# Scores of the first eight attention jobs in the float32 mode, weights in two strided transfers, and early v on GpSimd's queue

## The chip, the cores and the metric

The program runs on one NeuronCore of a Trainium2 chip. Its engines are PE (TensorE: matmuls; PEld are its weight loads), DVE (VectorE), ACT (ScalarE), POOL (GpSimd) and SP (SyncE), and transfers are issued on the queues of SP, ACT and POOL. The metric is the device time of one execution in microseconds; the time before is 1215.47 us, the median of 3 runs (1214.58 to 1215.83).

## The reference

Causal attention with a decay, over 8 batches of 8 heads, 576 positions and head size 64, all in float32; then a two-layer MLP with a squared ReLU on the 4608 tokens of width 512.

```python
scores = scale * np.matmul(q, k.transpose(0, 1, 3, 2))
cum = np.cumsum(np.log(np.clip(f, 0.0001, 1.0)), axis=-1)
scores = np.where(causal, -1e9, scores + cum[:, :, :, None] - cum[:, :, None, :])
attn = np.exp(scores - np.max(scores, axis=-1, keepdims=True))
attn = attn / (np.sum(attn, axis=-1, keepdims=True) + 1e-09)
x = np.matmul(attn, v)          # to [tokens, 512]
h = np.maximum(x @ w_in, 0.0)   # w_in 512 x 2048
out = h * h @ w_out             # w_out 2048 x 512
```

## The kernel before, in words

**Precision.** PE multiplies in one pass in a rounded mode (float32r) or, more slowly, in float32. Most products are made as three rounded ones: each operand is split into an upper (rounded) part and the rest, and upper x rest, rest x upper and upper x upper are added up in PSUM. The rounding copies and the subtractions that make the parts are work for ACT, DVE and POOL.

**Attention jobs** (the function `job`). Jobs 0 to 7 ("LOW") take two heads each of batches 0 and 1, and of them the first 256 positions. Jobs 8 to 23 ("HIGH") take one head each of the same batches, positions 256 to 575. The other 48 jobs ("FULL") take one whole head. A job loads q and k (`load`, ACT's queue) into a buffer, `raw`; copies q and k rounded to `r2` (c1) and `kl0` (c2), and, as the second operand pair, to `r1` and `l2` (c3, c4), which also get the rests from the subtractions s1, s2 (L607). `rows` brings the two parts of the cumulated decay by SP's queue. A rounded product of q and k (L687) gives each row's maximum on DVE (L695); the maximum goes as a column through a transfer on SP's queue (`up<-tcol`, L704) into a further row of the operand, so that the scores come out of PE with decay and maximum already in them: L739 (upper parts, with the three extra rows) and L743 (the rests, 128 rows). ACT takes the exponential (L749), POOL zeroes what lies above the diagonal (L752, the mask). In heads below `NWHOLE` the probabilities go into one float32 matmul with v (L824, which the profile shows as two records); in the others they are split (L777 on ACT, L780 on DVE) and go into three (L827, L828, L829). `finish` gathers the denominators of two jobs (`cmp<-den`, L901), inverts them on DVE (L905, L906), and spreads them by two more transfers.

**Weights** (`weight`). w_in and w_out come in 16 pieces each of 128 x 512 float64 numbers; a piece is loaded as int32 by POOL's queue (L420) and turned into float32 by one step on ACT (L423) and four on DVE (L427 to L444), then split into upper (L309, `w<-osb`) and rest (L452, the last step). The buffers of pieces 17 to 31 hold operands and v of the first jobs before.

**MLP** (`chunk`, `mlp`). 18 chunks of 256 tokens, 16 steps each. A chunk's x is split (L977, L983); a step is 12 matmuls of 256 columns (L1020), on ACT the ReLU (L1026) and the rounded square (L1035), a square (L1030 on ACT or L1032 on DVE), the rest (L1038 on DVE) and 6 matmuls of 512 columns (L1049). Chunks 0 and 1 start while weights still arrive: step n needs weights 2n and 2n+1.

**What sets the order.** All work is entered in a planner (class `Order`) with a priority, its needs, its buffers, and one or more engines with estimated costs; the planner runs through it in estimated time, takes for each engine the earliest, and writes down the order. Each engine then runs in exactly that order, and waits if an input is late. `SLACK` is a margin that the planner leaves behind each result, by the engine of the step that uses it. `job_prio` and `weight_prio` give the priorities.

Of the kernel before, what the change touches and what calls it, by code (L numbers as in the profile page):

```python
# [9 lines left out]
F32 = mybir.dt.float32  # L10
# [84 lines left out]
class Order:  # L95
# [6 lines left out]
    SLACK = {"PE": 250.0, "DVE": 200.0, "ACT": 200.0, "POOL": 200.0, "SP": 200.0}  # L102
# [19 lines left out]
    def run(self):  # L122
# [10 lines left out]
        while ready:  # L133
            best = {}
            for op in ready:
# [6 lines left out]
                else:  # L142
                    way = None
                    for w in op.ways:
# [4 lines left out]
                        if way is None or start + busy < way[0] + way[1][1]:  # L149
                            way = start, w  # L150
                    start, w = way
# [15 lines left out]
            if e in queue and path == "dma":  # L167

                queue[e] = max(queue[e], start + 600) + lag
                end = queue[e] + 1900  # L170
# [44 lines left out]
def decay_attention_relu2_kernel(  # L215
# [40 lines left out]
    NWHOLE = 16  # L256
# [15 lines left out]

# [61 lines left out]
    spare_v = []  # L334
    for i in (17, 18, 19):
        x = spare(i, F32)[:, :12 * (D + 2)].rearrange("p (g i j d) -> p g i j d", g=3, i=2, j=2)
        spare_v += [x[:, g] for g in range(3)]
    spare_v = spare_v[:NLOW]
# [71 lines left out]
    def weight(i):  # L410
# [7 lines left out]
        def stage(e):  # L418
            raw_w[i] = wk.tile([P, 2 * DM], I32, name=f"w{i}", bufs=1)
            nc.gpsimd.dma_start(out=raw_w[i], in_=(w_in, w_out)[i % 2][i // 2].bitcast(I32))  # L420
# [40 lines left out]
        elif 20 <= i < 24:  # L461
            after += [(x, g) for x in splits for g in range(RAWS)]
# [3 lines left out]
        add(w("stage"), [dma(8 * P * DM, "POOL")], stage, after, prio=p)  # L466
# [56 lines left out]
    def job(g):  # L523
# [37 lines left out]
        def rows(e):  # L561
# [4 lines left out]
            elif g == 0:  # L566
                for i, c in enumerate(cum):
                    nc.sync.dma_start(out=kl0[D + i:D + i + 1, :2 * QA].bitcast(F32), in_=c[:2, :QA])
# [52 lines left out]
        rp = [("ch", QA), ("cl", QA)] if g == 0 else [("cum", 0), ("cum", 1)]  # L621
        add(("c1", g), [act(nq)] if kind != LOW and b < 2 else [dve(nq)], c1, start, take=[operands], give=give, prio=p)
        add(("rows", g), [dma(20000, "SP", 1 if g else 2)], rows, [("c1", g)] + rp, prio=p)
        add(("c2", g), [act(nk)] if b < 2 else [dve(nk), act(nk)], c2, [("load", g), ("c1", g)], give=give, prio=p)
        add(("c3", g), [act(nk), dve(nk)], c3, [("load", g), ("c1", g)], give=give, prio=p + 0.1)
# [520 lines left out]
```

## Time and profile before

| | |
|---|---|
| median of 3 runs | 1215.47 us |
| profiled execution: its time, its span | 1220.14 us, 1218.4 us |
| busy in the span: PE, DVE, ACT, POOL | 1165.4, 790.8, 724.4, 381.0 us |
| first matmul, first MLP matmul | 9.94 us, 63.77 us |
| last weight ready (last L452 starts) | 247.4 us |

Times are in microseconds unless marked ns. A row of windows gives the stretch, its length, the busy time of PE, PEld, DVE, ACT and POOL with their instruction counts, the granted PE clock (1.00 is full), the busy share of the 16 DMA engines and GB/s; a stretch before the first change of the clock is given as 1.00 whatever it was. A row of the timeline gives start, duration, engine, line, operation, output<-input, shapes, and in brackets the idle time before it and what ended it. A group's row gives count, busy time, mean ns of one, and idle time before it. Matmuls overlap: one's duration is longer than what it adds to PE; the chain of waits counts only what it adds.

### The profile page before, as it was taken

How to read it: one execution, taken by the hardware profiler on the slowest of the kernel's cores; microseconds unless marked ns; L12 is line 12 of the kernel's file. 1: busy time of each engine (PE TensorE's matmuls, PEld its weight loads, DVE VectorE, ACT ScalarE, POOL GpSimd, SP SyncE). 2: the span in 40 equal slices, each digit the busy share in tenths (PEclk: the TensorE clock that was granted, in tenths of full speed). 3: DMA queues.
4: the chain of work that ended last, by engine and by line, in shares of the span. 5: the costliest groups of instructions: out<-in, count | busy, mean ns of one | idle time of the engine just before them, and what ended most of it. 6: DMA issues, size and time to landing. Idle time of an engine off the chain costs nothing.

```text
span 1218.4 us, 23217 instructions
## 1 busy us (share of the span) xinstructions
PE 1165.4 (96%) x7600; PEld 1038.7 (85%) x7600; DVE 790.8 (65%) x2211; ACT 724.4 (59%) x1859; POOL 381.0 (31%) x568
## 2 busy tenths in 40 slices
PE   4679998999999999999999999999999999999998
PEld 4558776789998898999999998899998999999997
DVE  7689988968877677777657674467656753233332
ACT  3566766556766666767777674477746763333232
POOL 3223321245444344544444442045423510000000
PEclk9689999999999999999999999999999999999999
DMA  3654554321222112222212212012211200000000
GB/s 80 140 129 121 143 154 113 87 77 43 65 50 62 40 41 59 47 64 47 59 42 59 42 43 58 19 41 43 69 31 44 47 28 11 18 19 11 8 19 18
DMA packets 122354, 69.85 MB, mean 57 GB/s; under 512 B 101914, under 2 KB 106042, under 8 KB 122234
## 3 DMA queue, kind: packets, MB, share of 16 engines
q10 hardware_dynamic: 53760, 31.47, 10.5%
q1 hardware_dynamic: 63866, 20.12, 7.5%
q0 software_dynamic: 4608, 16.78, 4.4%
q8 instruction: 61, 1.00, 0.3%
q14 instruction: 59, 0.48, 0.1%
HBM read 58.14 MB, written 9.88 MB: 56 GB/s over the span
## 4 chain that ended last, share of the span: by engine, by line
PE 85%; DMA 6%; DVE 4%; ACT 2%; issue 1%; POOL 1%; SPq 0%; ACTq 0%; POOLq 0%; DVEq 0%
PE bank L1049 31%; PE bank L1020 30%; PE bank L739 4%; PE bank L687 4%; PE bank L743 4%; PE bank L824 3%; PE bank L829 3%; PE bank L828 3%; PE bank L827 3%; DMA den<-rdr 2%; DMA cmp<-den 1%; DMA rdr<-cmp 1%; DMA up<-tcol 1%; DVE bank L695 1%; POOL pl L752 0%
## 5 line engine op out<-in xcount | busy, mean ns | idle before, releaser
L1049 PE MATMUL bank<-w,gh 128*128 128x512 f32 x1152 | 413.5, 400 | 1.9 <-DVE w L452 1.9
L1020 PE MATMUL bank<-xh,w 128*128 128x256 f32 x2304 | 324.4, 283 | 2.5 <-DVE xh L977 1.1
L1020 PEld LDWEIGHTS bank<-xh,w 128*128 128x128 f32 x2304 | 302.3, 189 | 13.7 <-DVE xh L977 1.3
L1026 ACT ACTIVATE r<-bank 128x256 f32<-128x256 f32 x288 | 110.2, 383 | 243.3 <-PE bank L1020 220.7
L1049 PEld LDWEIGHTS bank<-w,gh 128*128 128x128 f32 x1152 | 218.0, 189 | 41.8 <-DVE w L452 2.3
L1049 PE MATMUL bank<-w,gl 128*128 128x512 f32 x576 | 228.6, 397 | 0.3 <-DVE gl L1038 0.3
L1032 DVE TENSOR_TENSOR g<-r 128x256 f32<-128x256 f32 x191 | 82.9, 434 | 174.6 <-ACT r L1026 173.3
L1020 PE MATMUL bank<-xl,w 128*128 128x256 f32 x1152 | 182.0, 280 | 0.9 <-DVE xl L983 0.9
L752 POOL TENSOR_SCALAR_AFFINE_SELECT p<-p 128x128 f32<-128x128 f32 (+1 forms) x240 | 84.3, 353 | 307.3 <-ACT p L749 302.0
L695 DVE CUSTOM_DVE_ANT_0 bank<-bank,mz 128x448 f32<-128x448 f32 (+4 forms) x320 | 137.1, 431 | 66.5 <-PE bank L687 64.9
L780 DVE TENSOR_TENSOR pl<-p,ph 128x320 fp32r<-128x320 f32 (+3 forms) x240 | 147.9, 625 | 39.5 <-ACT ph L777 38.4
L1038 DVE TENSOR_TENSOR gl<-g,gh 128x256 fp32r<-128x256 f32 x288 | 139.6, 485 | 51.9 <-ACT g L1030 20.3
L1020 PEld LDWEIGHTS bank<-xl,w 128*128 128x128 f32 x1152 | 155.3, 189 | 1.3 <-DVE xl L983 1.3
L607 POOL TENSOR_TENSOR st<-qkraw,up 64x576 fp32r<-64x576 f32 x96 | 146.2, 1523 | 27.3 <-issue 5.4
L749 ACT ACTIVATE p<-bank 128x320 f32<-128x320 f32 (+4 forms) x288 | 110.0, 389 | 56.5 <-DVE pl L780 30.6
L739 PE MATMUL bank<-up 67*128 67x192 f32 (+3 forms) x364 | 121.8, 335 | 20.4 <-DMA up<-tcol 10.3
L1035 ACT ACTIVATE gh<-r 128x256 fp32r<-128x256 f32 x288 | 120.1, 417 | 31.6 <-PE bank L1049 11.6
L777 ACT CAST ph<-p 128x320 fp32r<-128x320 f32 (+3 forms) x240 | 106.2, 446 | 49.0 <-POOL p L752 27.6
L687 PE MATMUL bank<-up 66*128 66x448 f32 (+1 forms) x352 | 112.1, 322 | 13.0 <-DMA up<-w 9.9
L1049 PEld LDWEIGHTS bank<-w,gl 128*128 128x128 f32 x576 | 109.4, 190 | 15.1 <-DVE gl L1038 1.5
L743 PE MATMUL bank<-st 128*128 128x192 f32 (+3 forms) x364 | 109.3, 302 | 0.0
L739 PEld LDWEIGHTS bank<-up 67*128 67x128 f32 (+1 forms) x364 | 68.5, 188 | 31.5 <-DVE cmp L905 7.2
(102 smaller groups left out, 1612.5 us busy)
## 6 DMA issues: line engine op xcount, KB each, us to landing
qkraw<-in_qk ACTq DMA_DIRECT2D x48, 288.0 KB
v<-in_v ACTq DMA_DIRECT2D x64, 160.0 KB
out<-osb SPq DMA_DIRECT2D x35, 256.0 KB
w<-in_w_in POOLq DMA_DIRECT2D x16, 512.0 KB, 4.4
w<-in_w_out POOLq DMA_DIRECT2D x16, 512.0 KB, 4.6
den<-rdr SPq DMA_DIRECT2D x48, 144.0 KB
up<-tcol SPq DMA_DIRECT2D x232, 0.5 KB
qkraw<-in_qk ACTq DMA_DIRECT2D x11, 224.0 KB
```

The costliest lines, as they stand in the source:

```text
L607: (nc.vector if e == "DVE" else nc.gpsimd).tensor_tensor(out=out, in0=in0, in1=in1.bitcast(F32), op=ALU.subtract,)
L687: nc.tensor.matmul(ps.tile[:m, :n], r2[:D + 2, o + q0:o + q0 + m], kl0[:D + 2, o + k0:o + k0 + n], start=True, stop=True,)
L695: nc.vector.tensor_tensor_reduce(out=ps.tile[:m, :n], in0=ps.tile[:m, :n], in1=mz[:m, mo:mo + n], op0=ALU.add, op1=ALU.min, scale=-1.0, sc ...
L739: nc.tensor.matmul(ps.tile[:kn, :n], kl0[:D + 3, o + k0:o + k0 + kn], r2[:D + 3, o + q0:o + q1], start=True, stop=False,)
L743: nc.tensor.matmul(ps.tile[:kn, :n], l2[:, o + k0:o + k0 + kn], r1[:, o + q0:o + q1], start=False, stop=True,)
L749: nc.scalar.activation(out=pt.tile[:kn, :n], in_=ps.tile[:kn, :n], func=AF.Exp, scale=SCALE)
L780: nc.vector.tensor_tensor(out=pl.tile[:kn, :n], in0=pt.tile[:kn, :n], in1=ph.tile[:kn, :n].bitcast(F32), op=ALU.subtract,)
L1020: nc.tensor.matmul(ph.tile[:, :T], w[:, s, cc], x[:, cc, :], start=(cc == 0 and k == 0), stop=(cc == NCC - 1 and k == 2),)
L1026: nc.scalar.activation(out=r.tile, in_=ph.tile[:, :T], func=AF.Relu)
L1035: nc.scalar.activation(out=gh.tile, in_=r.tile, func=AF.Square)
L1038: nc.vector.tensor_tensor(out=gl.tile, in0=g.tile, in1=gh.tile.bitcast(F32), op=ALU.subtract)
L1049: nc.tensor.matmul(po, x[:, ts], w[:, s], start=(fc == 0 and k == 0), stop=(fc == NF - 1 and k == 2),)
```

## The change

1. **Scores of jobs 0 to 7.** c3, c4, s1 and s2 are left out. A score is a float32 matmul of the loaded q and k (64 rows, L768 of the changed kernel) and a rounded one of the three extra rows alone (L772). The maxima still use the rounded copies. `raw` is held until the scores are done.
2. **Weights** load in two transfers a piece, each of two runs of 1024 B a partition: 64 issues on POOL's queue rather than 32 of one 4096 B run.
3. **v of jobs 0 to 7**: six transfers on POOL's queue, each with one block of 128 positions of six heads (the last two with four), rather than 16 on ACT's queue, and entered with an earlier priority and without the old waits.
4. `NWHOLE` goes from 16 to 20: heads 16 to 19 (FULL) use the unsplit probabilities.
5. **The planner**: larger slacks, more slack behind the denominators' gather (1500) and the maxima's transfers (600 for 300), new priorities, decay rows of job 1 straight from SBUF (`DIRECT`), and a handicap of 450 for DVE wherever a step may run on ACT or DVE (`FAVOUR`); more steps have that choice.

```diff
-    SLACK = {"PE": 250.0, "DVE": 200.0, "ACT": 200.0, "POOL": 200.0, "SP": 200.0}
+    SLACK = {"PE": 350.0, "DVE": 300.0, "ACT": 300.0, "POOL": 200.0, "SP": 200.0}
+    FAVOUR = {"PE": 0.0, "DVE": 450.0, "ACT": 0.0, "POOL": 0.0, "SP": 0.0}
...
-                        if way is None or start + busy < way[0] + way[1][1]:
-                            way = start, w
+                        done = start + busy + self.FAVOUR[e]
+                        if way is None or done < way[2]:
+                            way = start, w, done
...
-    NWHOLE = 16
+    NWHOLE = 20
+    DIRECT = 2
+    SLACK_G, SLACK_C = 1500, 600
     def weight_prio(i):
-        return (14.9 if i < 4 else 16.9) + 0.8 * i
+        return (15.4 if i < 4 else 17.4) + 0.8 * i
...
-            return 12 + 2 * (g - NLOW)
-        return (30 if g < NLOW + BE * H else 98) + g - NLOW - H
+            return 8 + 2.5 * (g - NLOW)
+        return (25 if g < NLOW + BE * H else 98) + g - NLOW - H
...
-            nc.gpsimd.dma_start(out=raw_w[i], in_=(w_in, w_out)[i % 2][i // 2].bitcast(I32))
+            for x in range(2):
+                o, w = (
+                    a.rearrange("p (n x k) -> p n x k", n=2, x=2)[:, :, x]
+                    for a in (raw_w[i], (w_in, w_out)[i % 2][i // 2].bitcast(I32))
+                )
+                nc.gpsimd.dma_start(out=o, in_=w)
...
-            elif g == 0:
+            elif g < DIRECT:
...
-        add(("c3", g), [act(nk), dve(nk)], c3, [("load", g), ("c1", g)], give=give, prio=p + 0.1)
-        add(("c4", g), [act(nq), dve(nq)], c4, [("load", g), ("c1", g)], give=give, prio=p + 0.1)
+        if kind != LOW:
+            add(("c3", g), [act(nk), dve(nk)] if b < 2 else [act(nk)], c3, [("load", g), ("c1", g)], give=give, prio=p + 0.1)
+            add(("c4", g), [act(nq), dve(nq)] if b < 2 else [act(nq)], c4, [("load", g), ("c1", g)], give=give, prio=p + 0.1)
...
             def load_v(e):
-                for i, x in enumerate(heads):
-                    queue_of(e).dma_start(out=spare_v[g][:, i, :, :D], in_=v[x][:, :QA // P])
+                n = min(6, 2 * (NLOW - g))
+                for j in range(QA // P):
+                    nc.gpsimd.dma_start(
+                        out=spare_v[g // 3][:, :n, j, :D], in_=v[2 * g:2 * g + n, :, j].rearrange("h p d -> p h d"),
+                    )
...
                 r2, kl0, r1, l2 = sets()
+                if kind == LOW:
+                    nc.tensor.matmul(
+                        ps.tile[:kn, :n], raw.tile[:, i, 1, k0:k0 + kn], raw.tile[:, i, 0, q0:q1],
+                        start=True, stop=False,
+                    )
+                    nc.tensor.matmul(
+                        ps.tile[:kn, :n], kl0[D:D + 3, o + k0:o + k0 + kn], r2[D:D + 3, o + q0:o + q1],
+                        start=False, stop=True,
+                    )
+                    return
...
-                add(key, [act(n)] if c < 2 else [dve(n)], upper, need, take=[] if keys else [xs[c]], prio=p)
+                add(key, [act(n), dve(n)], upper, need, take=[] if keys else [xs[c]], prio=p)
```

The order shows how the planner moves things. On GpSimd, right behind the set-up, before the change (`ph`, `pl` are the probabilities of a score's two halves, `w_` the buffers of weights):

```order
L370 MEMSET warm 128x1
L752 AFFINE_SELECT ph_219<-ph_219 128x128
L752 AFFINE_SELECT pl_224<-pl_224 128x128
L752 AFFINE_SELECT ph_238<-ph_238 128x128
L752 AFFINE_SELECT pl_245<-pl_245 128x128
```

and now (L657 loads v, L432 a weight, x2 stands for two instructions):

```order
L376 MEMSET warm 128x1
L657 DMA w_83<-in_v 128x6x64 x2
L657 DMA w_84<-in_v 128x6x64 x2
L432 DMA w_210<-in_w_in 128x2x256 x2
L432 DMA w_221<-in_w_out 128x2x256 x2
L790 AFFINE_SELECT ph_225<-ph_225 128x128
L790 AFFINE_SELECT pl_231<-pl_231 128x128
L432 DMA w_238<-in_w_in 128x2x256 x2
```

Four v transfers and the first two weights now stand ahead of the first mask; before, the first weights came behind ten masks.

On DVE, jobs 0 and 1, behind the decay's first part, before (`st` holds the second operand pair, ISA rows are a maximum and the reading of its result):

```order
L309 CAST st_77<-qkraw 64x512 x2
L607 TENSOR_TENSOR st_77<-qkraw,up_71 64x512 x2
L388 TENSOR_TENSOR w_82<-xt_89,w_81 64x320
L695 ISA bank_175,tcol_177<-bank_175,mz 128x256
L695 ISA tcol_177 128x1
L309 CAST up_72<-w_160 64x512
L695 ISA bank_179,tcol_177<-bank_179,mz 128x128
L695 ISA tcol_177 128x1
L309 CAST st_78<-w_160 64x512 x2
```

and now:

```order
L394 TENSOR_TENSOR w_82<-xt_89,w_81 64x320
L316 CAST up_72<-w_157 64x512
L722 ISA bank_168,tcol_174<-bank_168,mz 128x256
L722 ISA tcol_174 128x1
L722 ISA bank_176,tcol_174<-bank_176,mz 128x128
L722 ISA tcol_174 128x1
L722 ISA bank_181,tcol_174<-bank_181,mz 128x256
```

The copies and subtractions between the maxima are gone.

On PE, the scores of job 0, before and then now (`qkraw` is the loaded q and k):

```order
L739 MATMUL bank_202<-up_71 128x256
L743 MATMUL bank_202<-st_77 128x256
L687 MATMUL bank_205<-up_72 128x256
L739 MATMUL bank_211<-up_71 128x128
L743 MATMUL bank_211<-st_77 128x128
```

```order
L714 MATMUL bank_207<-up_72 128x128
L768 MATMUL bank_215<-qkraw 128x256
L772 MATMUL bank_215<-up_71 128x256
L768 MATMUL bank_227<-qkraw 128x128
L772 MATMUL bank_227<-up_71 128x128
```

L768 and L772 take the places of L743 and L739, and now all four maxima of job 1 stand ahead of job 0's first score.

More of the change, by code (lines that the diff above doesn't have):

```diff
@@ L461, in weight @@
         elif 20 <= i < 24:
-            after += [(x, g) for x in splits for g in range(RAWS)]
+            after += [("score", g, len(jobs[g]["units"]) - 1) for g in range(NLOW)]
+            after += [(x, g) for x in splits for g in range(NLOW, RAWS)]
         elif i >= 24:
@@ L641, in job @@
+            if g == first:
+                add(
+                    ("v", g), [dma(400000, "POOL", 2)], load_v,
+                    [("v", g - 1) if g else ("load", 0)], prio=p - 2,
+                )
+            else:
+                add(("v", g), [("SP", 0, 0, None)], lambda e: None, [("v", first)], prio=p)
         else:
```

59 lines of the change are left out of this document (33 added, 26 removed).

## The prediction

> **What bounds the kernel now.** I read the windows first, by stage:
>
> ```profile
> 0.00:64.00 64.00, 37.31 (x159) 30.43 (x160) 46.63 (x140) 30.27 (x73) 19.37 (x58) 0.84 0.49 114
> 64.00:250.00 186.00, 168.23 (x957) 136.50 (x956) 163.17 (x417) 119.53 (x301) 52.71 (x99) 0.94 0.44 120
> 250.00:1000.00 750.00, 746.07 (x5121) 679.19 (x5120) 510.34 (x1472) 506.62 (x1321) 307.49 (x411) 1.00 0.21 49
> 1000.00:1218.40 218.40, 213.78 (x1369) 192.60 (x1367) 70.66 (x183) 67.98 (x166) 1.42 (x1) 1.00 0.04 14
> ```
>
> After the length come busy PE, weight load, DVE, ACT, POOL, then clock and DMA. From 250 us on PE is busy 959.9 of 968.4 us: only fewer matmuls could shorten that stage. Before 250 us PE idles 44.5 us. What it waits for there is read next, with the stretch up to the last weight:
>
> ```profile
> L452 DVE TENSOR_TENSOR w<-osb,w x32: 666/684/778, 55.3 to 247.4; 128x512 fp32r<-128x512 f32 x32
> 0.00:247.40 247.40, 202.94 (x1096) 164.64 (x1096) 207.51 (x554) 147.81 (x368) 69.48 (x156) 0.92 0.46 120
> 33.62 0.59 SPq L901 DMA_DIRECT2D cmp<-den  x1
> 40.58 0.17 DVE L905 TENSOR_SCALAR cmp<-cmp 128x8 f32<-128x8 f32 x1 [4.07 <-DMA cmp<-den]
> 40.87 0.55 PE L739 MATMUL bank<-up 67*128 67x256 f32 x1 [4.85 <-DVE cmp L905]
> ```
>
> L452 is the last step in preparing a weight; the 32 weights come out of DVE between 55.3 and 247.4 us, and until then each new MLP step needs a weight just made. DVE is busy 207.5 of those 247.4 us and idle 39.9, the longest single wait being the 4.07 us for the denominators, behind which PE stood 4.85 us. So I take 247.4 us, the end of the weights, as the end of the start-up; 971.0 us of PE-bound work follow (1165.4 - 202.9 = 962.5 busy).
>
> **The change, part by part.** *DVE.* A first-eight job (two heads) loses two copies of q, k (c3, c4) and two subtractions (s1, s2), each 512 columns:
>
> ```profile
> L607 DVE TENSOR_TENSOR w<-w,w 64x512 fp32r<-64x512 f32 x8 | 5.5, 682 | 0.1
> L309 DVE CAST w<-w 64x512 fp32r<-64x512 f32 x11 | 4.6, 414 | 0.2
> L309 DVE CAST w<-osb 128x512 fp32r<-128x512 f32 x14 | 6.1, 437 | 0.1
> L309 DVE CAST st<-qkraw 64x320 fp32r<-64x320 f32 x5 | 1.7, 332 | 0.0
> L1038 DVE TENSOR_TENSOR gl<-g,gh 128x256 fp32r<-128x256 f32 x288 | 139.6, 485 | 51.9 <-ACT g L1030 20.3 <-ACT gh L1035 19.2 <-PE bank L1049 0.5
> L977 DVE CAST xh<-xt 128x256 fp32r<-128x256 f32 x40 | 12.2, 328 | 2.6 <-PE bank L1020 2.6
> ```
>
> Counted in the order up to the last L452: 16 subtractions fewer (16 x 0.682 = 10.9 us), 18 casts of 512 columns fewer (7.5), 8 weight casts now on ACT (3.5), 5 short and 2 long key casts fewer (about 2.5), 17 small chunk steps (L977 and the differences behind it) fewer (about 5 at 0.3), 2 L1038 fewer (1.0); five more maxima and two long subtractions come in (about 5). Sum: -25 us, 207.5 to 182.5.
>
> *PE.* A score becomes one float32 matmul on raw q, k plus a three-row one, where L739 and L743 were two one-pass ones. The chain shows what each adds to PE, the timeline the clock:
>
> ```profile
> 118.35 0.09 PE bank L739
> 118.44 0.11 PE bank L743
> 118.78 1.42 PE bank L1020 x12
> 120.20 0.54 PE bank L824 x2
> 32.31 0.28 PE L743 MATMUL bank<-w,w 128*128 128x256 f32 x1
> 41.22 0.41 PE L743 MATMUL bank<-st 128*128 128x256 f32 x1
> 44.31 0.41 PE L743 MATMUL bank<-st 128*128 128x128 f32 x1
> ```
>
> L824 is the kernel's present float32 form, two records a matmul: 0.54 us for 320 columns, 0.43 for 256 against 0.12 (1.42 / 12) for a one-pass matmul. A unit of 256 columns costs 0.31 us more, one of 128 half of it; 16 of each: +7.5 us at full clock. At the clock of 41.22 us, where L743 takes 0.41 rather than 0.28, the streaming part doubles: +15. I take 7.5, since these matmuls fill PE more densely, and keep 15 for the range. The Trainium skill ("TensorE: Matmul & The Clock Gate", Part 1) has the array fall to half clock after some 3.4 us idle and return after as long of sustained work. The trace agrees on the fall (4.85 us idle, then 0.41) and not on the return: 3.4 us after the restart, at 44.31 us, even 128 columns still take 0.41. By the page the price is 7.5, by these rows nearer 15.
>
> *Four more heads (16 to 19) with one float32 probability matmul instead of three split ones.* The three lines take 8.4% of the chain for 48 heads:
>
> ```profile
> PE bank L1049 31%; PE bank L1020 30%; PE bank L739 4%; PE bank L687 4%; PE bank L743 4%; PE bank L824 3%; PE bank L829 3%; PE bank L828 3%; PE bank L827 3%; DMA den<-rdr 2%; DMA cmp<-den 1%; DMA rdr<-cmp 1%; DMA up<-tcol 1%; DVE bank L695 1%; POOL pl L752 0%
> L780 DVE TENSOR_TENSOR pl<-p,ph 128x320 fp32r<-128x320 f32 (+3 forms) x240 | 147.9, 625 | 39.5 <-ACT ph L777 38.4
> L1032 DVE TENSOR_TENSOR g<-r 128x256 f32<-128x256 f32 x191 | 82.9, 434 | 174.6 <-ACT r L1026 173.3
> L309 ACT CAST st<-qkraw 64x576 fp32r<-64x576 f32 x67 | 44.9, 670 | 1.6 <-issue 0.6
> L1030 ACT ACTIVATE g<-r 128x256 f32<-128x256 f32 x97 | 39.6, 409 | 6.2 <-DVE gl L1038 4.3 <-DVE pl L780 1.0 <-ACT r L1026 0.3
> 700.00:720.00 20.00, 20.00 (x145) 18.55 (x144) 13.12 (x38) 16.02 (x43) 10.75 (x14) 1.00 0.21 50
> ```
>
> At about 3 x 3% of 1218.4 us that is 2.3 us a head (the page rounds); in float32 1600 columns at 0.54 / 320 are 2.7. So +0.4 each, +2 us, in the PE-bound part. DVE loses 24 splits (L780, 15 us) where it is 68% busy: nothing on the path.
>
> *DVE to ACT.* The new preference moves 182 of the 191 squares (L1032) to ACT: 74 us at 0.409. 75 chunk casts (25 us at 0.328) and some 50 copies of q and k (30 at 0.6) follow, 24 splits go. ACT grows by some 120, from 724 to about 845 us; in the PE-bound part, less what falls into the start and the tail, from 68% to about 80% busy. The last row is 20 us with ACT at 80% and PE at 20.00: that load alone costs PE nothing. If the cover fails, each 1% of PE idle in 971 us is 9.7; I put 2.
>
> *Weights in two transfers each:* 32 more issues of about 0.57 us on GpSimd (381 us busy of 1218): hidden after the start. More, smaller packets move the same bytes; DMA is busy 0.49 of the start, and hides them. *v:* 16 issues leave ACT's queue and six enter GpSimd's, ahead of weights 0 and 1 and of the first masks:
>
> ```profile
> 6.10 0.10 POOL L370 MEMSET warm<- 128x1 f32 x1
> 16.13 0.29 POOL L752 TENSOR_SCALAR_AFFINE_SELECT ph<-ph 128x128 f32<-128x128 f32 x1 [9.94 <-ACT ph L749]
> 29.08 0.72 POOL L420 DMA_DIRECT2D w<-in_w_in  x1
> 29.80 0.54 POOL L420 DMA_DIRECT2D w<-in_w_out  x1
> 30.33 0.53 POOL L420 DMA_DIRECT2D w<-in_w_in  x1
> w<-in_w_in POOLq DMA_DIRECT2D x16, 512.0 KB, 4.4
> 0.00:30.00 30.00, 14.10 (x53) 12.02 (x54) 23.47 (x66) 10.34 (x22) 9.31 (x36) 1.00 0.35 79
> ```
>
> GpSimd had nothing from 6.2 to 16.1 us; eight issues of 0.53 to 0.72 end at 10.4 to 12. No row shows a v transfer there: it has 768 pieces (six heads by 128 partitions) to a weight's 128, so one issue lies between 0.53 (all fixed) and 3.2 (all by piece), and up to 4.4, the median from a weight's issue to its landing, if each waits for the one ahead to land. I take it near the bottom, by the rows of the same engine, and no wait. If that cover is gone, the first masks are late (rival B). With weights asked for at about 9 instead of 29 us DVE has their work early, in time it idled; and the plan now puts the denominators' step later in DVE's order, so the 4.07 us wait should shrink.
>
> **Sum.** If DVE's 39.9 us idle stayed, the weights would end at 182.5 + 39.9 = 222 us: the lower bound unless idle shrinks. If instead PE kept its idle time, they would end at 247.4 + 9 = 256, as PE does about 9 us more work ahead of that point (7.5 here, 2 in attention moved ahead of it). PE's idle came mostly from waiting on what DVE does late, so I go near the first: 227. Then 971.0 + 2 + 2 - 2 (moved ahead): 973. Span 1200, 18 shorter. The profiled execution took 1220.14 us (span 1218.4); the median of the runs shown is 1215.47, 4.7 below it. So 1200 + 1.7 - 4.7 = **1197 us**.
>
> **Rivals.** *A. More relief (0.10).* The stalls go and PE stays at full clock: DVE idle falls from 39.9 to about 25, weights end at 208, time 1178. For it: the 4.07 us wait; against: PE then has 203 + 9 us of work in 208 us, and only full clock makes that fit.
> *B. GpSimd's queue (0.11), slower.* The v issues are long, and the first masks, the first probabilities and, in order, PE wait behind. The place is the eight issues between 6.2 us and the mask at 16.1; the start slips by 8x - 9.9 us for a mean issue of x. At 3.2 it slips 16 and the time is 1213, at 4.4 it slips 25 and the time is 1222: from x = 3.5 on the 18 us are gone. For: 768 pieces; against: the three weight issues in a row of 0.72, 0.54, 0.53 us. The Trainium skill ("SBUF — State Buffer", section "SBUF: two separate sides") lets a DVE copy in a two-port mode lock GpSimd out of writing descriptors, a 0.62 us transfer becoming 3.1. By that figure the eight issues would end at 31 us and the time be some 15 us longer, 1212; here GpSimd's issues took 0.53 to 0.72 beside a DVE busy 23.47 of the first 30 us, so the trace does not bear it out.
> *C. The start does not shorten (0.12).* Float32 scores at half clock (+15) and the tiny transfers' latency set the pace, DVE's saved time becomes idle time: weights end at 247 to 256, time 1217 to 1226. For it: the half clock still there at 44.31 us; against: the 25 us less on DVE.
> *D. ACT becomes the bound (0.06).* PE idles 2% of 971 us more, 19 us: 1216. Against it stands the 700 to 720 row.
>
> The forecast has 0.61, its own range 1186 to 1209. The range of 8 in 10 reaches nearly to A's time and over most of B, C and D: 1181 to 1220. A measurement of this kernel can tell 0.2%, 2.4 us, from no change. Faster: 0.61 + 0.10 + a part of B = 0.76; same: 0.08, from B, C, D; slower 0.16.
>
> **What would show it.** Right: the last L452's successor (same step) at 220 to 235 us with DVE busy about 183 us by then; the first weight made before 35 us; a float32 score adding about 0.43 us for 256 columns; PE still above 98% after it. Wrong: GpSimd's v issues above 3 us and a first mask past 20 us (B); the weights' end at 245 us or later with DVE more idle than 55 us (C); PE idle after the weights grown by over 10 us, released by ACT (D); or an end of the weights as forecast and a rest above 985 us, which none of these explains.

## The result: 1.7% slower, and the profile after

The changed kernel takes 1236.1 us (median of 4 runs, 1234.5 to 1238.4) where the kernel before takes 1215.3 (4 runs, 1214.6 to 1215.8): a ratio of 1.0168, 95% interval 1.0155 to 1.0181. Forecast were 1197 us and 1181 to 1220. Below, a ratio is always a kernel's time over that of the kernel before on the same chip, with its 95% interval.

The profiled execution took 1234.49 us (span 1232.8). First the view of one line, the last weight step (L452 before, L464 now), with the first and last start:

```profile
L464 DVE TENSOR_TENSOR w<-osb,w x32: 673/686/778, 50.2 to 267.9; 128x512 fp32r<-128x512 f32 x32
```

Then the windows up to that last start and behind it; after the length stand busy PE, weight load, DVE, ACT and POOL, then clock and DMA:

```profile
0.00:267.90 267.90, 241.21 (x1140) 175.90 (x1141) 189.06 (x500) 160.31 (x394) 95.22 (x193) 1.00 0.45 112
267.90:1232.80 964.90, 956.99 (x6467) 868.48 (x6465) 483.51 (x1344) 652.26 (x1759) 284.15 (x400) 1.00 0.17 41
```

The weights end at 267.9 us, 20.5 later than before; the rest takes 964.9, 6.1 less. So the loss lies in the start-up: its 20.5 us less the 6.1 are the 14.4 us by which the two spans differ. (The medians differ by 20.8: the profiled execution of the kernel before was 4.8 us above its median, that of the changed one 1.6 below.) There PE was busy 202.9 us and is now busy 241.2 (+38.3); its idle time fell from 44.5 to 26.7. DVE, which I had as the limit, is busy 18 us less and idle 78.8 us of 267.9.

The start-up has two parts, cut by the first MLP matmul (L1020 before, L1064 now). Here is that matmul in PE's timeline of the changed kernel:

```profile
100.46 2.05 PE L1064 MATMUL bank<-xh,w 128*128 128x256 f32 x8
```

And windows about it:

```profile
20.00:25.00 5.00, 0.00 (x0) 0.00 (x0) 0.00 (x0) 0.33 (x1) 2.12 (x3) 1.00 0.57 170
30.00:100.00 70.00, 69.67 (x173) 39.61 (x173) 31.95 (x106) 30.68 (x75) 17.68 (x43) 1.00 0.31 79
90.00:100.00 10.00, 10.00 (x26) 5.54 (x24) 4.69 (x15) 5.29 (x14) 2.78 (x7) 1.00 0.35 98
100.00:110.00 10.00, 10.00 (x61) 9.07 (x61) 8.75 (x22) 8.07 (x23) 2.43 (x5) 1.00 0.19 51
100.50:267.90 167.40, 161.17 (x942) 129.85 (x941) 146.36 (x365) 121.45 (x307) 63.81 (x118) 1.00 0.49 122
```

Before, this matmul started at 63.8 us, so the first part is 36.7 us longer; the second takes 167.4 us instead of 183.6, 16.2 less. From 30 to 100 us PE reads busy 69.67 of 70 us, and has 26 matmul records in the last ten of them, against 61 in the ten behind (a float32 matmul makes two records). The clock column says 1.00, but a profile has no clock record before the first change, and the first here is the rise at 103.2 us. That PE ran at half clock until then is told by the durations: L772 of 256 columns takes 0.57 us below and 0.38 in a window that a record gives as full clock (with v by ACT, shown further down), L768 1.22 and 0.70. A second profile of the same kernel (the repeat in the first experiment) has the records: half clock from 45.4 to 100.0 us. PE's timeline of the changed kernel for two score units (256 and 128 columns):

```profile
83.74 1.22 PE L768 MATMUL bank<-w 64*128 64x256 f32 x2
84.89 0.57 PE L772 MATMUL bank<-w,w 3*128 3x256 f32 x1
85.39 0.58 PE L714 MATMUL bank<-up 66*128 66x256 f32 x1
...
86.76 0.79 PE L768 MATMUL bank<-w 64*128 64x128 f32 x2
87.48 0.47 PE L772 MATMUL bank<-w,w 3*128 3x128 f32 x1
87.88 0.64 PE L714 MATMUL bank<-up 66*128 66x320 f32 x1
```

And that of the kernel before, also at half clock (its records give half from 37.3 to 57.8 us):

```profile
53.28 0.55 PE L739 MATMUL bank<-up 67*128 67x256 f32 x1 [1.77 <-DVE cmp L905]
53.63 0.41 PE L743 MATMUL bank<-st 128*128 128x256 f32 x1
53.85 0.31 PE L739 MATMUL bank<-up 67*128 67x128 f32 x1
53.95 0.41 PE L743 MATMUL bank<-st 128*128 128x128 f32 x1
54.17 0.52 PE L739 MATMUL bank<-w,w 67*128 67x256 f32 x1
```

From start to start the two units take 1.65 + 1.12 = 2.77 us now and 0.57 + 0.32 = 0.89 before: 1.88 us more a pair, 30 us for the 16 pairs of the first eight jobs, if all of them ran at half clock in both kernels. Counted record by record, by what each adds to PE's busy time, the scores of these jobs take 44.4 us instead of 13.3: 31.1 of the 38.3 us.

The second new thing is on GpSimd, whose timeline begins so:

```profile
6.00 1.00 POOL L657 DMA_DIRECT2D w<-in_v  x1
10.08 0.84 POOL L657 DMA_DIRECT2D w<-in_v  x1 [3.08 <-issue]
14.19 0.83 POOL L657 DMA_DIRECT2D w<-in_v  x1 [3.27 <-issue]
18.71 0.83 POOL L657 DMA_DIRECT2D w<-in_v  x1 [3.68 <-issue]
22.22 1.42 POOL L432 DMA_DIRECT2D w<-in_w_in  x2 [2.69 <-issue]
23.64 0.70 POOL L432 DMA_DIRECT2D w<-in_w_out  x1
25.63 0.73 POOL L432 DMA_DIRECT2D w<-in_w_out  x1 [1.29 <-issue]
26.37 0.30 POOL L790 TENSOR_SCALAR_AFFINE_SELECT ph<-ph 128x128 f32<-128x128 f32 x1
```

PE's timeline right behind that mask:

```profile
26.72 1.12 PE L868 MATMUL bank<-ph,w 128*65 128x256 f32 x2 [6.82 <-POOL ph L790]
```

The v issues stand 4.1 to 4.5 us apart; the first mask comes at 26.37 us (16.13 before), and PE waits 6.82 us for it.

### The profile page after: what moved, and what is told of

The parts are those of the page before. It is cut to its first block, busy times and chain, and to the rows that moved or that the text cites. A ratio compares the mean times of both kernels' runs of the same rounds, so it can differ in the third digit from the quotient of the medians.

```text
span 1232.8 us, 22940 instructions
## 1 busy us (share of the span) xinstructions
PE 1198.2 (97%) x7604; PEld 1044.4 (85%) x7604; DVE 672.6 (55%) x1842; ACT 812.6 (66%) x2152; POOL 379.4 (31%) x593
## 5 line engine op out<-in xcount | busy, mean ns | idle before, releaser
L1064 PE MATMUL bank<-xh,w 128*128 128x256 f32 x2304 | 322.3, 282 | 1.6 <-ACT r L1070 0.8
L1064 PEld LDWEIGHTS bank<-xh,w 128*128 128x128 f32 x2304 | 302.5, 189 | 11.5 <-ACT r L1070 1.0
L1082 DVE TENSOR_TENSOR gl<-g,gh 128x256 fp32r<-128x256 f32 x288 | 148.8, 517 | 264.7 <-ACT g L1074 250.3
L1064 PE MATMUL bank<-xl,w 128*128 128x256 f32 x1152 | 181.9, 280 | 0.8 <-DVE xl L1027 0.8
L790 POOL TENSOR_SCALAR_AFFINE_SELECT p<-p 128x128 f32<-128x128 f32 (+1 forms) x220 | 71.9, 329 | 309.2 <-ACT p L787 300.0
L824 DVE TENSOR_TENSOR pl<-p,ph 128x320 fp32r<-128x320 f32 (+3 forms) x220 | 134.1, 614 | 49.5 <-ACT ph L821 48.0
L1064 PEld LDWEIGHTS bank<-xl,w 128*128 128x128 f32 x1152 | 155.4, 189 | 1.1 <-DVE xl L1027 1.1
L622 POOL TENSOR_TENSOR st<-qkraw,up 64x576 fp32r<-64x576 f32 x88 | 133.0, 1511 | 41.3 <-DVE up L316 14.0
L714 PE MATMUL bank<-up 66*128 66x448 f32 (+1 forms) x352 | 115.9, 335 | 16.2 <-DMA up<-w 13.3
L821 ACT CAST ph<-p 128x320 fp32r<-128x320 f32 (+3 forms) x220 | 97.5, 446 | 44.9 <-PE bank L873 14.9
L787 ACT ACTIVATE p<-bank 128x320 f32<-128x320 f32 (+4 forms) x264 | 101.2, 389 | 31.2 <-DVE pl L824 16.5
L777 PE MATMUL bank<-up 67*128 67x320 f32 (+2 forms) x348 | 116.6, 335 | 1.0 <-ACT den L901 0.5
L1074 ACT ACTIVATE g<-r 128x256 f32<-128x256 f32 x279 | 113.2, 406 | 1.1 <-DVE gl L1082 0.6
L781 PE MATMUL bank<-st 128*128 128x320 f32 (+2 forms) x348 | 101.8, 294 | 0.0
L714 PEld LDWEIGHTS bank<-up 66*128 66x128 f32 x352 | 66.0, 190 | 22.8 <-issue 14.5
```

What stands on the lines that cost most here:

```text
L622: (nc.vector if e == "DVE" else nc.gpsimd).tensor_tensor(out=out, in0=in0, in1=in1.bitcast(F32), op=ALU.subtract,)
L714: nc.tensor.matmul(ps.tile[:m, :n], r2[:D + 2, o + q0:o + q0 + m], kl0[:D + 2, o + k0:o + k0 + n], start=True, stop=True,)
L777: nc.tensor.matmul(ps.tile[:kn, :n], kl0[:D + 3, o + k0:o + k0 + kn], r2[:D + 3, o + q0:o + q1], start=True, stop=False,)
L781: nc.tensor.matmul(ps.tile[:kn, :n], l2[:, o + k0:o + k0 + kn], r1[:, o + q0:o + q1], start=False, stop=True,)
L824: nc.vector.tensor_tensor(out=pl.tile[:kn, :n], in0=pt.tile[:kn, :n], in1=ph.tile[:kn, :n].bitcast(F32), op=ALU.subtract,)
L1064: nc.tensor.matmul(ph.tile[:, :T], w[:, s, cc], x[:, cc, :], start=(cc == 0 and k == 0), stop=(cc == NCC - 1 and k == 2),)
```

## The experiments

**1. One half of the change undone at a time.** Theory 1 after reading the traces: GpSimd's queue and the float32 scores each cost, and add up. In these kernels v goes by ACT's queue, or the first eight jobs' scores are split as before, or both.

```diff
 # v by ACT
-                    nc.gpsimd.dma_start(out=spare_v[g // 3][:, :n, j, :D], in_=...)
+                    nc.scalar.dma_start(out=spare_v[g // 3][:, :n, j, :D], in_=...)
-  ("v", g), [dma(400000, "POOL", 2)], load_v, [... ("load", 0)], prio=p - 2,
+  ("v", g), [dma(400000, QUEUE, 2)], load_v, [... ("load", NPAIR - 1), ("rows", 0)], prio=p,
 # split scores
-        if kind != LOW:      # c3, c4, s1, s2 and the wait for them
+        if True:
-                if kind == LOW:      # the float32 score
+                if False:
```

> The changed kernel, with the six-head v transfers of the first jobs issued on ACT's queue instead of GpSimd's. Theory 1 (two causes that add: the queue makes the first mask 10 us late, and float32 scores run at half clock for some 70 us): the first mask comes back from 26.4 to about 16 us, PE's 6.82 us wait goes, the stretch of float32 scores stays at half clock; weights end some 8 to 10 us earlier, at about 250, time 1226. Theory 2 (the late queue alone is the cause; with an earlier start the clock rises as it did before): weights end at 225 to 235, time 1197 to 1207. Theory 3 (the half clock alone is the cause, and the late mask is absorbed): weights end at 256 to 260, time 1233 to 1236.

> The changed kernel, with the scores of the first eight jobs as before the change: copies and differences of q and k, two rounded one-pass matmuls, no float32 score; v stays on GpSimd's queue. Theory 1 (queue and half clock add): the clock reaches full within 40 us of the start as in the kernel before, but the first mask stays at about 26 us and DVE has its 25 us back: weights end at 250 to 257, time 1222 to 1229. Theory 2 (the queue alone): no gain from the split, time 1236 to 1245. Theory 3 (the half clock alone): time 1215 or less.

> The changed kernel with v of the first jobs on ACT's queue and the scores of the first eight jobs as before the change. What is left of the change is the planner's slack, landing and preference for ACT, other priorities, four more heads with one float32 probability matmul, and weights in two pieces. Theory 1 (the queue and the float32 scores carry the whole loss): 1210 to 1218. Rival (the new order of work or the pieces of weights cost something too): 1222 or more, with the weights' end at 250 us or later.

The changed kernel was timed once more on another chip:

> The changed kernel unchanged, on the chip of the three runs below, since the runs so far compare it across chips. Theory (v on GpSimd's queue costs 0.6% beside the float32 scores): ratio to the kernel before 1.015 to 1.018, above the 1.0106 of v on ACT's queue. Rival (that difference is one of chips): 1.010 to 1.012, and then the queue costs nothing beside the float32 stretch.

| first eight jobs' scores | v by GpSimd | v by ACT |
|---|---|---|
| float32 | 1.0168 (1.0155 to 1.0181); again 1.0154 (1.0125 to 1.0184) | 1.0106 (1.0075 to 1.0138) |
| split | 1.0017 (1.0001 to 1.0033) | 0.9934 (0.9909 to 0.9958) |

The float32 scores cost 1.4 to 1.7%, v on GpSimd 0.5 to 0.8%, and what is left of the change gains 0.4 to 0.7% (the repeats, here and in experiment 6, are counted in). With split scores the intervals of the two queues are apart; with float32 scores the repeat's overlaps that of v by ACT, so there the queue's part is uncertain. That both cost and about add up is as theory 1 had it, and theory 2 falls (1.0106 with v by ACT alone). Its sizes and its path were less good. With split scores 1.0017 is better than its 1222 to 1229 us (1.0055 or more) and worse than theory 3's 1215 or less, so the float32 scores cost more beside the late queue than theory 1 said; there the first mask came at 28.4 us, the weights ended at 259.6 (expected 250 to 257), and the clock was first full at 69.3 us, not within 40 (33.7 with v by ACT as well): the late queue alone holds the clock down too. With v by ACT the first mask came at 16.16 us and the first MLP matmul at 89.0, but the weights ended at 266.0, not about 250. The second part then took 177.0 us instead of 167.4: 4.6 of the 9.6 us are more PE work in it, 5.0 more idle time, in waits of less than 2 us each that I have not followed further.

**2. Each half alone on the kernel before.**

> The kernel before with one part of the change alone: float32 scores on q and k as loaded in the first eight jobs (no third and fourth copies, no differences), v on ACT's queue and everything else as it was. Theory (the float32 scores hold PE at half clock and cost PE 1.1 us more for each 256 columns and 0.8 for each 128, 16 of each, 30 us, of which DVE's 18 us less and PE's waits take part back): first MLP at 80 to 90 us instead of 63.8, ratio 1.010 to 1.018. Rival (in the old order of work DVE is the limit up to 247 us, and the float32 scores only use PE's waits): 0.995 to 1.004.

> The kernel before with one part of the change alone: v of the first eight jobs six heads a transfer, by GpSimd's queue. Theory (each issue waits for room, 4.1 to 4.5 us apart, so the first mask moves from 16.1 to about 24 to 28 us, PE waits 7 us, and DVE, the limit of the old start, loses part of that): 1.004 to 1.008. Rival (DVE has other work meanwhile and hides it): 0.998 to 1.002.

Float32 scores alone: 1.0255 (1.0229 to 1.0280), more than expected, with the first MLP matmul at 91.2 us instead of 63.8. A window while PE works on the first scores:

```profile
30.00:40.00 10.00, 10.00 (x27) 5.62 (x26) 2.24 (x10) 3.29 (x9) 3.42 (x8) 1.00 0.39 105
```

And that matmul in PE's timeline:

```profile
91.22 2.06 PE L1039 MATMUL bank<-xh,w 128*128 128x256 f32 x8
```

The rival, that DVE's limit would hide them, falls: DVE is busy 2.24 of 10 us there, and PE 10.00. GpSimd's v alone: 1.0072 (1.0046 to 1.0099), in the theory's range, with a first mask at 23.06 us (expected 24 to 28) and a wait of PE for it of 4.06 us (expected 7). In the changed order the float32 scores cost 1.4 to 1.7%, about 1% less than in the old one; which part of the new order does that is not shown.

**3. What spaces the issues on GpSimd.** The kernel holds 1024 bytes a partition for GpSimd's DMA descriptors; two kernels got 2048, the changed one and the one with split scores.

```diff
-    nc = bacc.Bacc("TRN2", ..., dynamic_dma_scratch_size=1024)
+    nc = bacc.Bacc("TRN2", ..., dynamic_dma_scratch_size=2048)
```

> The changed kernel with twice the scratch for GpSimd's DMA descriptors (2048 bytes a partition instead of 1024), v still on GpSimd's queue. Theory R (a v transfer of 768 pieces nearly fills the room for descriptors, and the next issue stands until it has drained): the first two or three v issues follow each other within 1.0 us, the first mask comes at 16 to 20 us instead of 26.4, and the time stands to the kernel before as with v on ACT's queue, about 1.011. Rival (an issue waits for the one ahead to land, or writes its descriptors slowly, whatever the room): issues 4.1 to 4.5 us apart as now, first mask at about 26, ratio about 1.017.

> The changed kernel with the scores of the first eight jobs as before the change, v on GpSimd's queue, and twice the scratch for GpSimd's DMA descriptors. Theory R (the room for descriptors made v's issues slow): the first mask at 16 to 20 us instead of 28.4, ratio 0.993 to 0.998, as with v on ACT's queue, against 1.0017 with the small scratch. Rival (v on GpSimd costs by something else too): 0.999 to 1.003.

GpSimd's timeline of the changed kernel with 2048 bytes:

```profile
6.00 1.83 POOL L657 DMA_DIRECT2D w<-in_v  x2
10.05 0.83 POOL L657 DMA_DIRECT2D w<-in_v  x1 [2.21 <-issue]
11.41 0.82 POOL L657 DMA_DIRECT2D w<-in_v  x1 [0.53 <-issue]
12.22 0.70 POOL L432 DMA_DIRECT2D w<-in_w_in  x1
...
21.39 0.28 POOL L790 TENSOR_SCALAR_AFFINE_SELECT ph<-ph 128x128 f32<-128x128 f32 x1 [3.86 <-ACT ph L787]
```

The second issue now follows the first at once, 1.0 us behind it, and waits begin with the third. That is what theory R says (a transfer of 768 pieces fills most of the small room, and the next one stands until it drains), and not what its rival says; how much room a transfer takes was not measured. The first mask comes at 21.4 us, later than the 16 to 20 expected, and waits for ACT, not for the queue: the score ahead of it waited 3.65 us for the transfer of its decay rows (`w<-cum_dr`). The ratios are 1.0100 (1.0074 to 1.0125) and 0.9979 (0.9958 to 1.0000), 0.4 to 0.7% below the same kernels with the small room; the second lies at the upper edge of theory R's range (0.993 to 0.998).

**4. Why PE stays at half clock.** First, dummy matmuls in PE's idle time, so that it comes to the float32 stretch at full clock.

```diff
+   for _ in range(36):   # ahead of the first matmul; 30 ahead of the first L868
+       nc.tensor.matmul(ps.tile[:, :MW], mz[:, :P], mz, start=True, stop=True)
```

> The changed kernel, with 36 dummy bfloat16 matmuls of 448 columns on PE ahead of its first matmul and 30 more ahead of the first probability matmul, in the time in which PE waits anyway; nothing else is moved. It asks whether PE only starts the float32 stretch at half clock and cannot leave it, or whether that stretch itself brings the clock down. If it only cannot leave it: a float32 score of 256 columns takes about 0.6 us instead of 1.22, eight jobs that took 70 us take some 35 to 40, PE stands idle for weights then, and the time falls below the changed kernel's 1236, to 1205 to 1220. If the stretch itself brings the clock down: 1.22 us again from some point between 30 and 50 us on, time 1230 to 1238.

PE's timeline:

```profile
23.58 4.24 PE L871 MATMUL bank<-mz 128*128 128x448 bf16 x20
...
29.38 0.70 PE L771 MATMUL bank<-w 64*128 64x256 f32 x2
30.01 0.38 PE L775 MATMUL bank<-up 3*128 3x256 f32 x1
...
36.78 0.69 PE L874 MATMUL bank<-pl,w 128*65 128x128 f32 x2 [3.84 <-POOL pl L793]
```

Two of its windows, the third number from the end being the clock:

```profile
40.00:50.00 10.00, 10.00 (x27) 5.50 (x25) 3.72 (x13) 3.85 (x10) 2.57 (x6) 0.50 0.30 79
90.00:100.00 10.00, 10.00 (x27) 5.59 (x25) 4.92 (x16) 4.92 (x12) 2.78 (x7) 0.50 0.28 73
```

At full clock a float32 score of 256 columns takes 0.70 us, as expected. Then PE waits 3.84 us for a mask that stands behind the next two v issues, the clock falls at 34.4 us, and for 68 us it does not come back, with PE busy 10.00 of 10 in nearly all of it. The ratio is 1.0097 (1.0072 to 1.0123). The time is that of the second theory (the stretch itself brings the clock down), but its reason is not shown: the fall came in a wait, and what this run shows is that the stretch does not bring the clock back. The same with v by ACT:

> The changed kernel with v on ACT's queue, with 36 dummy bfloat16 matmuls of 448 columns ahead of PE's first matmul and 16 ahead of the first probability matmul. Reading so far: in windows of 3.41 us the clock rises after PE has streamed columns for 0.9 or more of the time at half clock, and falls after about half that share at full clock; the float32 stretch streams 0.55 to 0.75 at half clock, so it cannot rise, but at full clock it would stream enough to stay. Theory bistable: with v out of the way of the masks, the clock, once full, holds for 15 us or more of the stretch, and a float32 score of 256 columns takes 0.7 us there; the time is 0.995 to 1.005. Rival (waits at full clock open gaps that bring it down again): half clock again before 45 us and for most of the stretch; ratio 1.007 to 1.011.

The clock was full from 5.6 to 15.9, from 32.9 to 43.2 and from 46.6 to 50.0 us, ten of those together inside the stretch where I had asked for 15; 1.0118 (1.0098 to 1.0137), just above the rival's range. The rival holds. Next, two dummies of 448 columns ahead of each float32 score, and q and k in all 128 rows:

```diff
+   for _ in range(2):
+       nc.tensor.matmul(ps.tile[:, :MW], mz[:, :P], mz, start=True, stop=True)
    nc.tensor.matmul(ps.tile[:kn, :n], raw.tile[:, i, 1, k0:k0 + kn], raw.tile[:, i, 0, q0:q1], ...)
```

> The changed kernel with v on ACT's queue, and in it two dummy bfloat16 matmuls of 448 columns into the same bank ahead of each float32 score of the first eight jobs (64 in all, 12 us of PE at full clock, 24 at half). Theory F (the float32 stretch keeps the clock down since it holds too few one-pass full-array matmuls): with the fillers the clock comes back to full within the stretch, a float32 score of 256 columns takes about 0.6 us, and the eight jobs end by 75 us instead of 92; time 0.995 to 1.008 of the kernel before. Rival (the clock comes back for other reasons, such as the mix with the MLP's matmuls, or a fixed time): half clock as without them, the stretch longer by 15 to 24 us, ratio 1.015 to 1.03.

> The changed kernel with v on ACT's queue, and q and k of the first eight jobs loaded into both halves of the partitions (sixteen more transfers on SP's queue), so that the float32 score runs over 128 rows instead of 64. This counts q.k twice in those scores, so the numbers that come out are others. Theory rows (64 of 128 rows in use are too few for the clock to rise): the clock is full before 60 us and the stretch ends by 70 us. Rival theory mode (float32 matmuls of four passes keep it down however many rows): half clock up to 85 to 100 us as with v on ACT's queue, where the full clock came at 92.5.

With fillers the clock stayed at half until 61.2 us though PE read busy 10.00 of 10 from 20 to 60; the first MLP matmul moved from 89.0 to 109.2 us, ratio 1.0296 (1.0269 to 1.0323): the rival's time. The clock did come back within the stretch, from 61.2 to 74.9 us, and then was half again until 112.4, so theory F falls by its time and not by every sign. With 128 rows the clock was full from 41.7 to 48.5 and from 58.7 to 62.1 us only, and the first MLP matmul came at 86.5 us where theory rows had the stretch end by 70; 1.0079 (1.0049 to 1.0109) beside 1.0106 with 64 rows, where the clock was full from 48.4 to 51.8. Theory rows falls; the ratios tell nothing apart.

What fits all profiles is how many columns PE really streams. I counted column passes (columns of a matmul, times four for float32: in the kernel before, 320 float32 columns add 0.54 us at full clock and 256 one-pass columns 0.12, 3.6 times as much a column) in each window of 3.41 us, the step of the clock records, up to 250 us. In the 20 profiles of this study, a window with 3500 column passes or more was followed by one at full clock, and one with fewer by one at half clock, in 1408 of 1445 cases; of the 77 windows at half clock above the bound 65 were followed by full clock, of the 385 below it 11. (Most windows only repeat the clock of the one ahead, 1311 of 1445; of the 134 changes the rule has 115.) In the float32 stretch of the changed kernel each window from 31.6 to 96 us held 2304 to 3456. The dummies in a row give about 4000 a window at half clock; the two fillers lifted the stretch to some 2600 to 3100 only, up to the window of 3584 ahead of 61.2 us. This is a rule read off the profiles, and no run was made to break it.

**5. How much the small matmul behind each float32 score costs.** The decay, constant and maximum rows are put under q and k as loaded, so that one float32 matmul of 67 rows does it all.

```diff
-  nc.tensor.matmul(ps, raw.tile[:, i, 1, ...], raw.tile[:, i, 0, ...], start=True, stop=False)
-  nc.tensor.matmul(ps, kl0[D:D + 3, ...], r2[D:D + 3, ...], start=False, stop=True)
+  nc.tensor.matmul(ps, raw.wide[:D + 3, i, 1, ...], raw.wide[:D + 3, i, 0, ...], start=True, stop=True)
```

> The changed kernel with v on ACT's queue, and the decay rows, the constant rows and the maxima put under q and k as loaded, so that a score of the first eight jobs is one float32 matmul of 67 rows; the three-row matmul behind it goes, and ten more small transfers go on SP's queue. At half clock that matmul takes 0.50 us a score of 256 columns and 0.40 of 128, 16 of each: 14 us of a stretch that is 70 us long. Theory (the stretch at half clock sets the start, and PE sets the stretch): half clock stays, MLP begins at 75 to 80 us instead of 89, ratio 0.998 to 1.004. Rival (other engines or the small transfers set the stretch): MLP begins at 86 us or later, ratio 1.008 to 1.012.

1.0013 (1.0003 to 1.0023), first MLP matmul at 72.9 us instead of 89.0, weights' end at 243.5 instead of 266.0. The theory holds: PE sets the stretch, and taking the three-row matmuls out gives 0.9% against v by ACT alone. One point was better than expected: the clock was full for 10 us from 30.0, so a part of the gain is the clock's; how large a part is not told apart.

**6. What the rest of the change gains by.** With v by ACT and split scores, each weight goes in one transfer again, first planned anew, then with every engine's order kept; and the kernel before gets two pieces and nothing else.

```diff
-            for x in range(2):
-                ...
-                nc.gpsimd.dma_start(out=o, in_=w)
+            nc.gpsimd.dma_start(out=raw_w[i], in_=(w_in, w_out)[i % 2][i // 2].bitcast(I32))
```

> The changed kernel with v on ACT's queue, scores of the first eight jobs as before the change, and each weight in one transfer again. Theory (the gain of 0.7% that is left when the queue and the float32 scores are undone comes from the order of work and the preference for ACT): ratio to the kernel before the same 0.993, plus or minus 0.002. Rival (the two pieces carry that gain): 0.998 to 1.002; rival (they cost): 0.989 or less.

> As the kernel with v on ACT's queue, scores as before the change and each weight in one transfer, but planned as if each weight were two transfers, so that every engine's order is that of the same kernel with two pieces (0.993). Theory order (the two pieces won by moving the plan, not by their size): 0.991 to 0.996. Rival size (short pieces let small transfers through sooner): 0.998 to 1.002, with the weights' end some 3 us or more later than 246.5.

> The kernel before with each weight in two transfers of 1024-byte pieces and nothing else: every engine's order is word for word that of before. Theory size (short pieces let the small transfers of the start through sooner): 0.993 to 0.997. Rival (the pieces do nothing by themselves, and the 0.9934 against 0.9988 measured on two chips is scatter): 0.999 to 1.002. Rival (32 more issues of about 0.6 us hold up GpSimd's masks): 1.002 to 1.006.

> Again the changed kernel with v on ACT's queue and scores of the first eight jobs as before the change, beside the next one on one chip: ratio 0.991 to 0.996 as before, if that reading was no scatter; 0.997 to 1.000 if it was.

> Again the same with each weight in one transfer and every engine's order kept, beside the last one on one chip. Theory size: 0.004 to 0.007 above the last one. Rival scatter: within 0.002 of it.

Planned anew: 0.9998 (0.9978 to 1.0019), not the theory's 0.993, but the plan moved with the pieces; its start-up ended early, at 230.0 us, but 984.5 us followed, with 13.7 of them at half clock from 381.9 on, after waits of PE. With the order kept: 0.9988 (0.9970 to 1.0006), and on the second chip 0.9977 (0.9961 to 0.9993) beside 0.9955 (0.9938 to 0.9973) with two pieces: a difference of 0.0022, between the 0.004 of theory size and the 0.002 of scatter. The kernel before with two pieces: 1.0013 (0.9992 to 1.0034). So the pieces alone do nothing in the old order; in the new one 0.2 to 0.5% is seen, at the edge of what can be told. What the rest gains otherwise stays open between the plan, the four heads and the preference for ACT. With v by ACT, split scores and two pieces the kernel beats the kernel before as well as the changed one, at 0.9934 and 0.9955. Its windows:

```profile
0.00:246.52 246.52, 206.27 (x1122) 166.29 (x1122) 201.76 (x528) 169.48 (x415) 93.51 (x188) 0.94 0.50 124
246.52:1210.10 963.58, 958.75 (x6450) 870.76 (x6450) 470.36 (x1341) 649.78 (x1744) 283.38 (x399) 1.00 0.17 41
```

Its start-up ends where that of the kernel before does (246.5 us, 247.4 there), with 3.4 us more PE work done by then, and PE idles 4.8 us behind it instead of 8.5.

## Why the prediction was wrong, step by step

- **What bounds the kernel.** That 971 us behind the last weight are PE-bound was right: forecast 973, measured 964.9, PE idle 7.9 of them.
- **The float32 scores: the step that failed.** "I take 7.5, since these matmuls fill PE more densely, and keep 15 for the range." Measured were 31.1 us of PE's busy time, and by the pairs above 30 at half clock: twice the 15 that the range kept for half clock. At full clock 256 columns take 0.63 + 0.31 and 128 take 0.41 + 0.25 from start to start, in the kernel before 0.24 and 0.23. First PE's timeline with v by ACT, at full clock by the records (48.4 to 51.8 us):

```profile
49.53 0.70 PE L768 MATMUL bank<-w 64*128 64x256 f32 x2
50.16 0.38 PE L772 MATMUL bank<-up 3*128 3x256 f32 x1
50.47 0.65 PE L868 MATMUL bank<-ph,w 128*65 128x256 f32 x2
51.05 0.48 PE L768 MATMUL bank<-w 64*128 64x128 f32 x2
51.46 0.32 PE L772 MATMUL bank<-up 3*128 3x128 f32 x1
51.71 0.60 PE L868 MATMUL bank<-pl,w 128*65 128x128 f32 x2
```

  And PE's timeline of the kernel before, at full clock too (30.5 to 37.3 us):

```profile
32.19 0.28 PE L739 MATMUL bank<-w,w 67*128 67x256 f32 x1
32.31 0.28 PE L743 MATMUL bank<-w,w 128*128 128x256 f32 x1
32.43 0.22 PE L687 MATMUL bank<-up 66*128 66x128 f32 x1
32.49 0.27 PE L739 MATMUL bank<-w,w 67*128 67x128 f32 x1
32.60 0.28 PE L743 MATMUL bank<-w,w 128*128 128x128 f32 x1
32.72 0.33 PE L687 MATMUL bank<-up 66*128 66x256 f32 x1
```

  That is 1.13 us more a pair, 18 us in all. So the term was 2.4 times too small even at full clock: I took L824's 0.43 us for a float32 matmul of another shape (0.63), and the three-row matmul for as cheap as the L743 that it replaces (0.31 against 0.12). The clock did the rest, about 13 us. "Densely" was read as busy time, and busy time is not what brings the clock back: PE read busy 69.67 of 70 us at half clock. The Trainium skill ("TensorE: Matmul & The Clock Gate", Part 1) lets the clock return after some 3.4 us of sustained work; the traces agree only if work means column passes, with the bound of some 3500 in 3.41 us.
- **DVE's 25 us.** DVE was busy 18.4 us less up to the last weight, with the end 20 us later. The step that used it failed: "PE's idle came mostly from waiting on what DVE does late, so I go near the first", that is 227. The other bound, 256, was nearer in form (it starts from PE's work and idle time), with 9 us of added PE work in it, where 38.3 were added and 17.8 of idle went: 267.9. What set the end was PE's added work, not DVE.
- **v on GpSimd.** "I take it near the bottom, by the rows of the same engine, and no wait" failed. The rows were of weights with 128 pieces; eight issues from 6.00 to 26.37 us make a mean of 2.55 us, between the bounds. By rival B's form the start slips by 8 x 2.55 - 9.9 = 10.5 us, and the first mask is 10.2 later. The price on the kernel before, 0.72% or 8.8 us for a first mask 6.9 us later, is of that size. The lock of the Trainium skill ("SBUF — State Buffer", "SBUF: two separate sides") is not what made these issues slow: from 20 to 25 us DVE was busy 0.00, and the issue at 22.22 still had 2.69 us of waiting ahead of it. More room for descriptors took the wait ahead of the second issue away.
- **Weights in two pieces, ACT, four heads.** The 64 issues cost nothing that can be seen (1.0013 alone, 0.9992 to 1.0034). ACT is busy 652.3 of 964.9 us behind the last weight, and PE idles 7.9 there against 8.5: the preference for ACT is free, as forecast, and D is out. The 2 us for four heads can't be told: PE is busy 1165.0 us in the profile of the kernel with both halves undone, and 1165.4 before.
- **Rivals.** I gave B 0.11 and C 0.12 and priced each alone. Both came: the weights' end past 245 us with DVE idle 78.8 (C), the first mask past 20 us (B). C's upper time, 1226, and B's 10 us add up to the 1236 measured, but by luck: C had the float32 scores at 15 us where 31.1 were measured, and its other reason, the latency of tiny transfers, was not seen to set the pace. The second part of the start-up, 16.2 us shorter, and the rest, 6.1 shorter, are near the gain that I forecast, and the first part, 36.7 longer, takes it away. No run ties the 16.2 us to DVE's relief, though: in the kernel before with float32 scores alone, where DVE has that relief too, the second part takes 178.4 us, only 5.2 less than before, and with v by ACT and split scores 183.1.

## What to carry to other kernels

Price a matmul of a new type by a row with its own rows, columns and number of matmuls, and at the clock of the stage where it will stand; count column passes, not busy time, to judge whether the clock will rise there (a rule read off these profiles, not tested further). A transfer of many small pieces on GpSimd's queue should be priced by its pieces and by the room for descriptors, not by a transfer of large pieces on the same queue, and everything behind it on GpSimd moves with it. Where two rivals can come true together, price them together.

## What was not expected of the hardware

PE busy 69.67 of 70 us stayed at half clock, and so did other kernels with the same scores (until 99.9 us in the kernel before with these scores alone); 3500 column passes in 3.41 us tell full from half in 97% of the windows. A three-row one-pass matmul of 256 columns took 0.31 us at full clock behind a float32 one, where a 128-row one-pass matmul took 0.12. GpSimd issued v transfers of 768 pieces 4.1 to 4.5 us apart with 1024 bytes a partition for descriptors, and the first two 1.0 us apart with 2048.
